# Running TensorE's head inside a two-pass loop so that the next instruction block is touched early

## Chip, cores and metric

One core of one Trainium2 chip. The metric is the device time of one execution in microseconds (us).

## The reference, cut to what matters

The reference is one decode step of a transformer block for 8 sequences: adaptive layer norm, grouped-query attention over a cache of 8,192 keys, and a dense layer with squared relu.

```python
# B = 8, D = 512, Hq = 32, Hkv = 8, Sk = 8192, Dh = 128, F = 1792; everything bf16
mod = silu(c) @ w_mod                              # 6 modulation vectors
q = (layernorm(x) * (1 + ca) + sa) @ wq
p = softmax(q @ k_cache^T * Dh ** -0.5)            # k_cache, v_cache: 134 MB each
x = x + ga * ((p @ v_cache) @ wo)
h = layernorm(x) * (1 + cb) + sb
x = x + gb * (relu(h @ w1 + b1) ** 2 @ w2 + b2)
```

The two caches are 268 MB of the 284 MB that have to be read.

## The kernel before

All engines run a recorded list of operations. On TensorE, VectorE and ScalarE the work of one sequence (a "batch") is the body of a loop of eight passes. Ahead of the loop stands the engine's head (modulation, q projection), behind it the tail (the end of the last batch, `wo`, `w1`, `w2`). The sync engine issues the loads, unrolled, into a ring of four 4 MiB slots.

```python
def _looped(self, e, eng, passes):
    nc, per, pe = self.nc, self.per[e], self.LOOP[e]
    seen, first = {}, {}
    for o in self._part(e, None):                       # the head
        self._emit(eng, o, self._want(e, o, 0), seen)
    # ... cut: waits that lie outside the loop are emitted here
    with nc.Fori(0, passes, engines=[pe], head_slot={pe: 0} if e == "tensor" else None) as i:
        for j, o in enumerate(self._part(e, (0, "a"))):
            self._emit(eng, o, first["a", j], seen)
        with eng.If(i < passes - 1):                    # the last pass leaves part b out
            # ... cut: part b, a drain, the semaphores set back by one pass
    for o in self._part(e, "post"):                     # the tail
        self._emit(eng, o, self._want(e, o, passes - 1), after)
```

`head_slot` pins the loop's first instruction at a slot of a block of 256 instructions, so that nothing ahead of the loop can shift its body. On TensorE the head has about 200 instructions, the body about 1,700, the tail about 580.

The tail ends with the dense layer. The last two loads are 512 KB and 256 KB of `w2`:

```python
d_w2 = [dma("sync", s_w2[i], ...) for i, (a, z, j) in
        enumerate(((0, 4, 4), (4, 8, 4), (8, 12, 4), (12, 14, 2)))]
...
for f in range(FT):                                     # FT = 14
    for k in range(KT):                                 # KT = 4
        t = op("tensor", lambda e, f=f, k=k: e.matmul(
            yT_ps[:, k, :], W2v[:, f, k * 128:(k + 1) * 128], hidT[:, f, :],
            start=False, stop=(f == FT - 1), ...), [k_sq[f // 7], d_w2[f // 4]])
```

## Time and profile before

| | before |
|---|---|
| time, median of the runs ahead of the prediction | 669.88 us (669.33 to 670.03) |
| span of the profiled run | 667.6 us |
| bytes moved | 283.85 MB, 425 GB/s over the span |
| TensorE busy | 77% of the span |
| DMA hardware queue | 99.1% of the 16 DMA engines' span |

From the page of the kernel before, the span and the DMA queues (packets, MB, share of the 16 engines' span):

```profile
span 667.6 us, 15485 instructions
...
## 3 DMA queue, kind: packets, MB, share of 16 engines
q1 hardware_dynamic: 12116, 283.65, 99.1%
q8 instruction: 9, 0.15, 0.1%
```

Queue q1 is the kernel's own loads. Queue q8 carries instructions: nine packets of 16,384 bytes, each 1.02 to 1.10 us long. From the instruction records I work out when they come: the first begins after TensorE enters the loop, and the other eight each after TensorE has gone through another 256 of the recorded instructions that follow, counted in program order (the body has 1,696). So I read a packet as one block of 256 TensorE instructions, and speak of a boundary at each 256th and of the fetch that it triggers. That a fetch brings the block after the one just entered is my reading too: when a packet of pass 1 begins, TensorE has already begun 19 to 111 instructions behind the boundary.

The windows view of the kernel before (stretch and its length in us; busy time of each engine; the last three columns are TensorE's granted clock, the DMA share and GB/s):

```profile
27.00:105.00 78.00, 59.24 (x804) 41.17 (x804) 35.70 (x64) 31.52 (x35) 0.00 (x0) 0.89 1.00 425
339.00:417.00 78.00, 62.32 (x840) 41.86 (x840) 36.59 (x66) 31.52 (x35) 0.00 (x0) 0.89 1.00 432
646.00:668.00 22.00, 14.17 (x304) 9.47 (x296) 6.13 (x22) 0.64 (x2) 0.00 (x0) 0.72 0.73 291
```

In a batch of 78 us the DMA share is 1.00 and TensorE is busy for about 60 us. The waits view of the kernel before (us in total, times, longest) says the same from the other side:

```profile
PE PS L479 <- DMA ring<-in_A_k_cache_dram: 51.2, 9, 10.1
PE PS L616 <- DMA ring<-in_A_v_cache_dram: 45.9, 10, 6.5
```

TensorE waits for keys and values, not they for it. Two stretches remain, the start and the end. The timeline of TensorE at the start (start us, length us, what, and in brackets the idle time before it and what ended it):

```profile
4.52 0.29 PE L373 MATMUL PS<-IDENT,KTb 8*128 8x8 bf16 x4 [4.52 <-DVE KTb L369]
...
11.33 3.21 PE L398 MATMUL PS<-ring,KTb 128*32 128x512 bf16 x24
...
30.71 1.04 PE L479 MATMUL PS<-IDENT,ring 128*128 128x128 bf16 x8 [5.12 <-DMA ring<-in_A_k_cache_dram]
```

The end, from the timeline of the kernel before:

```profile
661.68 1.02 PE L751 MATMUL PS<-KTb,ring 128*128 128x8 bf16 x32 [0.98 <-DVE KTb L747]
...
663.57 1.01 PE L751 MATMUL PS<-KTb,ring 128*128 128x8 bf16 x24 [0.87 <-DMA ring<-in_B_w_dram]
```

The last 24 `w2` matmuls wait 0.87 us for data. What follows them takes 3 us (a VectorE step, transposes, a copy, the output). The critical view (the chain of work that ended last: start us, length us, what) shows that the last eight of them stand directly behind the landing of the last load:

```profile
649.42 14.74 DMA ring<-in_B_w_dram
664.16 0.05 issue
664.21 0.39 PE PS L751 x8
```

The trace also records every DMA packet. I read two things from these records, which no view of the profile prints. They are worked out, not lines of the profile.

```
instruction fetches, kernel before, us:
 31.80  42.42  50.93  69.86  77.61  86.85  102.89      652.52  661.23
last w2 landing, by engine, us (the six latest of 16; the very last is the engine of the 661.23 fetch):
 662.21 662.22 662.46 662.67 662.71                     663.74
```

The engine of the last fetch has its `w2` packets behind that fetch. It ends at 663.74 us, 1.0 us after all others. These are the landings of two tiles, engine by engine, as distance from a straight line of 9.7115 us a tile (worked out from the packet records); the fetch at 102.89 us lies between them:

```
tile 9,  us: 0.63 0.73 0.74 0.75 0.80 0.87 1.04 1.31 1.51 1.69 2.15 2.16 2.16 2.17      2.63 2.66
tile 10, us: 0.62 0.73 0.75 0.76 0.80      1.03 1.30 1.50 1.68 2.15 2.16 2.16 2.17 2.42 2.63 2.65
```

One engine has gone from 0.87 to 2.42 us, the others stand. A tile counts as landed when the last of its 16 engines is done: above, TensorE's last eight matmuls start at 664.21 us, although 15 engines had written their share by 662.71 us.

### The profile page before, as it was taken

To read this page: it belongs to the slowest core of one execution; us is meant where nothing else is said; L and a number is where in the kernel's file an instruction comes from. 1 tells how busy PE (TensorE), PEld (TensorE's weight loads), DVE (VectorE), ACT (ScalarE), POOL (GpSimd) and SP (SyncE) were. 2 spreads that over 40 slices of the span, in tenths; PEclk is the share of its full clock that TensorE was granted. 3 is DMA by queue.
4 is the path that set the end of the run, shared out by engine and by line. 5 is a ranking of instruction groups with operands and counts; after the bars stand their busy time and mean duration, and the time that the engine had idled before them with its cause. 6 is when DMAs were issued, how large, how long until landed. Compare 5 with 4: busy or idle time off the path is not lost.

```text
span 667.6 us, 15485 instructions
## 1 busy us (share of the span) xinstructions
PE 513.8 (77%) x7064; PEld 344.8 (52%) x7064; DVE 302.6 (45%) x571; ACT 258.7 (39%) x289; POOL 18.4 (3%) x76
## 2 busy tenths in 40 slices
PE   3493984898739985699848987499756998389885
PEld 2283731675328742577317853287425773177534
DVE  2262731566216651367314662166513673156722
ACT  2151640466105660266404662066502654046610
POOL 7300000000000000000000000000000000000000
PEclk9696997899969998699977999699987999779996
DMA  9999999999999999999999999999999999999996
GB/s 376 431 412 437 426 427 435 432 430 430 434 434 430 430 432 436 428 432 432 436 428 430 434 434 430 430 434 434 428 432 434 434 426 434 432 434 428 434 415 264
DMA packets 12176, 283.85 MB, mean 425 GB/s; under 512 B 1250, under 2 KB 1283, under 8 KB 3588
## 3 DMA queue, kind: packets, MB, share of 16 engines
q1 hardware_dynamic: 12116, 283.65, 99.1%
q8 instruction: 9, 0.15, 0.1%
q10 hardware_dynamic: 48, 0.02, 0.0%
q14 instruction: 3, 0.02, 0.0%
HBM read 283.66 MB, written 0.01 MB: 425 GB/s over the span
## 4 chain that ended last, share of the span: by engine, by line
PE 52%; DMA 37%; ACT 7%; DVE 2%; SPq 1%; issue 1%
PE PS L479 36%; DMA ring<-in_A_k_cache_dram 32%; PE PS L496 9%; ACT P_sb L562 5%; PE PS L616 2%; DMA ring<-in_B_w_dram 2%; DMA ring<-in_A_wq_dram 2%; PE PS L469 1%; SPq L659 1%; ACT KTb L484 1%; DVE O_sb L626 1%; PE PS L463 1%; PE PS L574 1%; DVE Pm L588 0%; PE PS L594 0%
## 5 line engine op out<-in xcount | busy, mean ns | idle before, releaser
L484 ACT ACTIVATE KTb<-PS 128x1024 bf16<-128x1024 bf16 x192 | 196.5, 1024 | 332.2 <-PE PS L479 332.2
L479 PE MATMUL PS<-IDENT,ring 128*128 128x128 bf16 x4096 | 267.4, 227 | 51.2 <-DMA ring<-in_A_k_cache_dram 51.2
L479 PEld LDWEIGHTS PS<-IDENT,ring 128*128 128x128 bf16 x4096 | 246.8, 102 | 99.6 <-DMA ring<-in_A_k_cache_dram 52.4
L486 DVE COPY KTb<-PS 128x1024 bf16<-128x1024 bf16 x320 | 210.1, 687 | 143.9 <-PE PS L479 141.8
L616 PE MATMUL PS<-ring,Pm 128*32 128x512 bf16 x992 | 70.4, 434 | 46.8 <-DMA ring<-in_A_v_cache_dram 45.9
L496 PE MATMUL PS<-KTb,Qb 128*32 128x512 bf16 x1024 | 78.8, 385 | 4.5 <-ACT KTb L484 4.5
L626 DVE CAST O_sb<-PS 128x512 bf16<-128x512 f32 x31 | 21.4, 692 | 126.7 <-PE PS L616 126.7
L616 PEld LDWEIGHTS PS<-ring,Pm 128*32 128x32 bf16 x992 | 26.8, 106 | 85.5 <-DMA ring<-in_A_v_cache_dram 54.4
L562 ACT ACTIVATE P_sb<-PS,negm 128x1024 bf16<-128x1024 f32 x32 | 35.2, 1112 | 20.2 <-DVE negm L557 20.2
L469 PE MATMUL PS<-ONES 128*128 128x512 f32 x80 | 42.1, 630 | 0.0
L574 PE MATMUL PS<-IDENT,P_sb 128*128 128x128 bf16 x256 | 19.9, 220 | 15.4 <-ACT P_sb L562 15.4
L588 DVE COPY Pm<-PS 64x512 bf16<-64x512 bf16 x48 | 20.2, 421 | 25.0 <-PE PS L574 24.5
L574 PEld LDWEIGHTS PS<-IDENT,P_sb 128*128 128x128 bf16 x256 | 14.4, 98 | 25.1 <-ACT P_sb L562 25.1
L463 PE MATMUL PS<-IDENT 128*128 128x512 bf16 x88 | 26.9, 380 | 0.0
L496 PEld LDWEIGHTS PS<-KTb,Qb 128*32 128x32 bf16 x1024 | 15.4, 94 | 21.1 <-ACT KTb L484 8.5
L503 DVE TENSOR_REDUCE m<-PS 128x1 f32<-128x512 f32 x32 | 22.0, 689 | 6.6 <-PE PS L496 6.6
L630 PEld LDWEIGHTS PS<-SEL,O_sb 128*128 128x128 bf16 x124 | 5.8, 97 | 30.5 <-DVE O_sb L626 30.5
L469 PEld LDWEIGHTS PS<-ONES 128*128 128x128 f32 x80 | 12.7, 190 | 10.6 <-issue 10.6
L630 PE MATMUL PS<-SEL,O_sb 128*128 128x8 bf16 x124 | 7.9, 169 | 12.4 <-DVE O_sb L626 12.0
L641 DVE TENSOR_TENSOR oTn<-PS,rinv 128x8 f32 x31 | 6.0, 194 | 14.9 <-PE PS L630 14.9
L463 PEld LDWEIGHTS PS<-IDENT 128*128 128x128 bf16 x88 | 7.7, 105 | 9.1 <-issue 7.2
L484 ACT ACT_TABLE_LOAD x8 | 10.3, 1283 | 3.2 <-issue 3.2
(132 smaller groups left out, 115.9 us busy)
## 6 DMA issues: line engine op xcount, KB each, us to landing
ring<-in_A_k_cache_dram SPq DMA_DIRECT2D x32, 4096.0 KB, 34.2
ring<-in_A_v_cache_dram SPq DMA_DIRECT2D x31, 4096.0 KB, 27.8
ring<-in_A_wq_dram SPq DMA_DIRECT2D x1, 4096.0 KB, 19.9
wo_sb<-in_A_wo_dram SPq DMA_DIRECT2D x1, 4096.0 KB, 47.6
ring<-in_w_mod_dram SPq DMA_DIRECT2D x1, 3072.0 KB, 10.3
ring<-in_A_v_cache_dram SPq DMA_DIRECT2D x1, 2048.0 KB, 22.6
ring<-in_B_w_dram SPq DMA_DIRECT2D x3, 512.0 KB, 19.4
ring<-in_B_w_dram SPq DMA_DIRECT2D x1, 1344.0 KB, 17.9
```

Of the source, the lines that this page charges most:

```text
L463: ts = [op("tensor", lambda e: e.matmul(bank(at).rearrange("p (a r) -> p a r", a=4), IDENT[:, :], rhs)) for _ in range(n)]
L469: ts = [op("tensor", lambda e: e.matmul(bank(at).rearrange("p (a r) -> p a r", a=4), ONES[:, :], rhs)) for _ in range(n)]
L479: t = op("tensor", lambda e, j=j, i=i: e.matmul(STG[j][:, i, :], src[:, 32 * k + 8 * j + i, :], IDENT[:, :], is_transpose=True), [loaded[n ...
L484: stg_free[j] = op("scalar", lambda e, j=j, dst=dst: e.activation(dst, STG[j], ACT.Copy), [t])
L486: stg_free[j] = op("vector", lambda e, j=j, dst=dst: e.tensor_copy(dst, STG[j]), [t])
L496: t = op("tensor", lambda e, hf=hf, q=q, rhs=rhs: e.matmul(PS[32 * q:32 * (q + 1), k, :], Qb[:, 2 * p + hf, :], rhs, start=(p == 0 and hf ...
L503: return op("vector", lambda e: e.tensor_reduce(m4[:, k:k + 1], bank(k), AX.X, ALU.max), [t])
L562: exps.append(op("scalar", lambda e, k=k: e.activation(P_sb[:, k, :, :, :], bank(k).rearrange("p (i x) -> p i x", i=8).unsqueeze(2).to_bro ...
L574: t = op("tensor", lambda e, k=k, i=i: e.matmul(STG[k][:, i, :], P_sb[:, k, i, :, :].rearrange("p h x -> p (h x)"), IDENT[:, :], is_transp ...
L588: done.append(op("vector", lambda e, dst=dst, frm=frm: e.tensor_copy(dst, frm), [t, k_pm]))
L616: t = op("tensor", lambda e, p=p, m=m, cg=cg, vt=vt, Obank=Obank: e.matmul(Obank[32 * cg:32 * (cg + 1), :], lhs[:, p, 32 * m:32 * m + 32], ...
L626: t = op("vector", lambda e, osb=osb, Obank=Obank: e.tensor_copy(osb, Obank), [t])
```

## The change

The intent: make TensorE enter the block of the loop's body before the head's work begins, so that the block after it is fetched early and not when the loop starts. For that the head stands in a loop of two passes. Pass 0 skips the head and jumps to the first slot of the next block (this is what the alignment does), from where the loop's branch goes back. Pass 1 runs the head. The main loop's first instruction moves from slot 0 to slot 16, as the closing instructions of the new loop now have the first slots of that block.

```diff
-        for o in self._part(e, None):
-            self._emit(eng, o, self._want(e, o, 0), seen)
+        if e == "tensor":
+            with nc.Fori(0, 2, engines=[pe]) as i:
+                with eng.If(0 < i):
+                    for o in self._part(e, None):
+                        self._emit(eng, o, self._want(e, o, 0), seen)
+                eng.addr_align(bass.FETCH_BLOCK_INSTRUCTIONS, offset=0, max_nops=0)
+        else:
+            for o in self._part(e, None):
+                self._emit(eng, o, self._want(e, o, 0), seen)
 ...
-        with nc.Fori(0, passes, engines=[pe], head_slot={pe: 0} if e == "tensor" else None) as i:
+        with nc.Fori(0, passes, engines=[pe], head_slot={pe: 16} if e == "tensor" else None) as i:
```

## The prediction

> **What bounds the kernel now.** The DMA stream. The page's part 3 gives the hardware queue 99.1% of the 16 engines' span; the windows view shows DMA share 1.00 at 425 to 432 GB/s in every batch, TensorE busy 59 to 62 of 78 us. A 4 MiB tile lands every 9.71 us. TensorE waits for it (waits view: 51 us before key transposes, 46 us before value matmuls), so TensorE work or a branch inside the loop is off the critical path. Critical are the stream and what follows its last byte: the last `w2` landing is written at 663.7 us, the last 24 matmuls start at 663.57 us, the span ends at 667.6 us.

> **What the change does.** No arithmetic, wait or kernel DMA is added or removed. TensorE gets about ten control instructions; the loop body moves from slot 0 to slot 16 of its block. I count about 1,700 instructions, 7 blocks of 256 in both versions. Pass one jumps over the head, enters the body's first block, and jumps back. TensorE has nothing to do until 4.5 us (timeline), so the pass is free there if it takes under 3 us.

> What moves is an instruction fetch. [...] 9 packets of 16,384 bytes, at 31.8, 42.4, 50.9, 69.9, 77.6, 86.8, 102.9, 652.5, 661.2 us, none in passes 2 to 8, so the loop stays resident [...]. Each is one packet on one busy engine. From neighbouring packets' ends I work out that it sets that engine back about 1.07 us (its landings' phase goes from 0.66 to 1.69 us at the first), for good. Seven engines carry one each by 103 us. The fetch at 661.2 us hits an engine of that slow group ahead of its last `w2` packets: it ends at 663.74 us, the next slowest at 662.71 us. So 1.0 us of fetch is critical at the end.

> Entering the body's block near 1 us should bring the 31.8 us fetch to about 2 to 3 us, as the stream starts (first packet 1.84 us). If the engine still has idle startup time then, and is the one that takes the 661.2 us fetch (eight fetches later; the phases permit it), the end comes up to 1.0 us earlier. If the stream already runs, the same work is only done earlier: nothing gained. Estimate: 0 to 1.0 us, mean 0.4 us.

> **Predicted time.** 669.4 us, 8 in 10 between 668.6 and 670.2 us. Chances: faster by over 2% 0.005, within 2% 0.99, slower by over 2% 0.005.

> **What would show it.** Still 9 or 10 TensorE fetches; the first near 2 to 3 us, none near 31.8 us; later ones within 1 us of before. Tiles still every 9.71 us. The last `w2` landing between 662.7 and 663.8 us; TensorE's last wait for `w2` 0.87 us or less. Busy times the same.

> **What would make it wrong.** If slot 16 pushed the loop out of residence, fetches would appear in each pass: about 56 more, each 1.07 us on one of 16 engines, some 4 us. If the jump back refetches blocks, a few more, under 1 us. If an extra fetch shifts the engines' order, the last may fall on another engine, up to 1 us either way.

The forecast's sum came to a gain of 0 to 1.0 us, mean 0.4 us, and so to 669.4 us, from the 1.0 us by which the engine of the last fetch ends behind the next (663.74 and 662.71 us). That a fetch would follow the entry into the block within 1 to 2 us was my own estimate; the trace of the kernel before has 4.3 us.

## The result

| | before | after |
|---|---|---|
| time, median of 4 runs | 669.86 us (669.33 to 670.03) | 669.61 us (669.29 to 670.03) |
| ratio | | 0.9998 (95%: 0.9981 to 1.0015) |
| span of the profiled run | 667.6 us | 667.5 us |
| instruction fetches | 9 | 9 |

A ratio here is the mean time of one kernel's fast runs over that of the other's of the same rounds, so it is not quite the ratio of the medians in the table. The two kernels cannot be told apart.

From the page of the kernel after, span and queues:

```profile
span 667.5 us, 15496 instructions
...
## 3 DMA queue, kind: packets, MB, share of 16 engines
q1 hardware_dynamic: 12116, 283.65, 99.1%
q8 instruction: 9, 0.15, 0.1%
```

The windows view of the kernel after, the same stretches:

```profile
27.00:105.00 78.00, 60.72 (x804) 42.29 (x804) 36.00 (x68) 31.73 (x36) 0.11 (x1) 0.89 1.00 426
339.00:417.00 78.00, 61.62 (x840) 41.08 (x840) 36.47 (x66) 31.54 (x35) 0.00 (x0) 0.91 1.00 431
646.00:668.00 22.00, 14.28 (x304) 9.59 (x296) 6.12 (x22) 0.64 (x2) 0.00 (x0) 0.69 0.72 289
```

The waits view of the kernel after (its line numbers are 7 higher):

```profile
PE PS L486 <- DMA ring<-in_A_k_cache_dram: 50.0, 9, 9.0
PE PS L623 <- DMA ring<-in_A_v_cache_dram: 45.3, 10, 6.5
```

The start of the kernel after, from its timeline:

```profile
4.52 0.29 PE L380 MATMUL PS<-IDENT,KTb 8*128 8x8 bf16 x4 [4.52 <-DVE KTb L376]
...
11.83 3.60 PE L405 MATMUL PS<-ring,KTb 128*32 128x512 bf16 x24 [0.66 <-DMA ring<-in_w_mod_dram]
...
31.26 0.50 PE L486 MATMUL PS<-IDENT,ring 128*128 128x128 bf16 x3 [5.04 <-DMA ring<-in_A_k_cache_dram]
```

The end of the kernel after, from its timeline:

```profile
661.73 1.05 PE L758 MATMUL PS<-KTb,ring 128*128 128x8 bf16 x32 [0.97 <-DVE KTb L754]
...
663.43 1.01 PE L758 MATMUL PS<-KTb,ring 128*128 128x8 bf16 x24 [0.65 <-DMA ring<-in_B_w_dram]
```

Its critical view ends in the same way:

```profile
649.55 14.47 DMA ring<-in_B_w_dram
664.02 0.05 issue
664.07 0.39 PE PS L758 x8
```

The first matmul starts at 4.52 us in both: the extra pass is hidden. But the `w_mod` matmuls now wait for data and start 0.5 us later, and so do the first key transposes. The packet records show why:

```
instruction fetches, kernel after, us:
  6.29  42.99  51.09  69.79  78.34  85.54  100.41      652.37  660.00
last landing of the first tile (w_mod), slowest engine:  before 10.73 us, after 11.36 us
last w2 landing, slowest engine:                         before 663.74 us, after 663.61 us
```

The fetch of 31.8 us is gone and one at 6.29 us has come in its place. The slowest landing of `w_mod` is 0.6 us later. I read that as the engine of the fetch, and the runs below agree: it is 11.28 to 11.47 us in the five kept traces with an early fetch and 10.56 to 11.17 us in the eight without. The records of TensorE's control instructions date the cause: the jump to the next block is issued at 1.36 us, the first instruction there runs at 1.72 us, pass 1 reaches the head at 2.3 us. From 1.72 us to the transfer it is 4.6 us. In the kernel before the loop is entered at 27.47 us and the fetch begins at 31.80 us, 4.3 us later. So the early fetch met a stream that had been running since 1.84 us.

### The profile page after: what moved, and what is told of

Read it like the earlier page. It is cut to its first block, busy times and chain, and to the rows that moved or that the text cites. A ratio compares the mean times of both kernels' runs of the same rounds, so it can differ in the third digit from the quotient of the medians.

```text
span 667.5 us, 15496 instructions
## 1 busy us (share of the span) xinstructions
PE 515.8 (77%) x7064; PEld 345.8 (52%) x7064; DVE 302.4 (45%) x571; ACT 258.9 (39%) x289; POOL 18.6 (3%) x76
## 2 busy tenths in 40 slices
DMA packets 12176, 283.85 MB, mean 425 GB/s; under 512 B 1250, under 2 KB 1283, under 8 KB 3588
## 3 DMA queue, kind: packets, MB, share of 16 engines
q1 hardware_dynamic: 12116, 283.65, 99.1%
## 4 chain that ended last, share of the span: by engine, by line
PE 52%; DMA 36%; ACT 7%; DVE 2%; SPq 2%; issue 1%
PE PS L486 36%; DMA ring<-in_A_k_cache_dram 32%; PE PS L503 9%; ACT P_sb L569 5%; PE PS L623 2%; DMA ring<-in_B_w_dram 2%; DMA ring<-in_A_wq_dram 2%; SPq L666 1%; PE PS L476 1%; ACT KTb L491 1%; DVE O_sb L633 1%; PE PS L470 1%; PE PS L581 1%; DVE Pm L595 1%; PE PS L601 0%
## 5 line engine op out<-in xcount | busy, mean ns | idle before, releaser
L486 PEld LDWEIGHTS PS<-IDENT,ring 128*128 128x128 bf16 x4096 | 247.5, 103 | 98.8 <-DMA ring<-in_A_k_cache_dram 51.2
```

The lines of the kernel that those rows point to most:

```text
L486: t = op("tensor", lambda e, j=j, i=i: e.matmul(STG[j][:, i, :], src[:, 32 * k + 8 * j + i, :], IDENT[:, :], is_transpose=True), [loaded[n ...
```

## The experiments

Theory A: the kernel is bound by the DMA stream and by what follows its last byte. An instruction fetch is work on one DMA engine (at the fetch of 102.89 us one engine's landing went from 0.87 to 2.42 us, the others stood). Moved, it is the same work at another time, and only the last fetch lies on the critical path. Rival B: the early fetch did gain something, and slot 16 or the extra pass gave it back. Rival C: the end is set by TensorE's own tail, not by the last fetch.

### Slot 16 alone

The kernel before, with one edit:

```diff
-head_slot={pe: 0}
+head_slot={pe: 16}
```

> The kernel before with only the loop's head moved from slot 0 to slot 16, no two-pass loop. Theory A (the fetch only moved: DMA stream bound, a fetch sets one DMA engine back by the same amount wherever it falls): 669.3 to 670.1 us, ratio 1.000, 9 fetch packets with the first near 31.8 us, last w2 landing 663.6 to 663.8 us. Rival B (the early fetch gained something near 0.5 us and slot 16 or the extra pass gave it back): slot 16 alone is slower by about 0.5 us, or the two-pass loop alone is (next run).

Measured: 669.55 us (669.37 to 670.45, 5 runs) against 669.44 us before, ratio 1.0002 (0.9989 to 1.0016). Nine fetches, the first at 31.9 us, last `w2` landing 663.84 us (just above the range expected). Slot 16 by itself costs nothing that five rounds can see. One thing moved: the seventh fetch came at 100.5 us and not at 102.9. With slot 16 it came at 100.3 to 101.5 us in all six kept traces. The block boundary falls 16 instructions earlier in the pass there, which may be the reason. But a run with slot 0 (the 16-row loads below) had it at 101.5 us too, so a part can be the run.

### The extra pass without its touch

The changed kernel, with one edit; pass 0 then ends in the head's own block:

```diff
-                eng.addr_align(bass.FETCH_BLOCK_INSTRUCTIONS, offset=0, max_nops=0)
```

> The changed kernel without the alignment in the first pass, so that pass ends in the head's own block and touches no other. Theory A: the first fetch is back near 31.8 us, the tiles' front (first w_mod matmul) back near 11.3 us instead of 11.8 us, and the time is still 669.3 to 670.1 us. Rival B: the pass without its touch costs about 0.5 us or more.

Measured: 669.80 us (669.46 to 669.84, 5 runs), ratio 1.0001 (0.9988 to 1.0015). The first fetch is back at 31.9 us, the `w_mod` matmuls start at 11.24 us again, and the slowest `w_mod` landing is back at 10.86 us (10.73 before, 11.36 after). So it is the touch, not the pass, that moves the fetch and sets one engine of the first tile back, and neither moves the time. Rival B falls as far as 0.15% can show: no part of the change costs or gains 1 us.

### Ten passes in place of two

```diff
-            with nc.Fori(0, 2, engines=[pe]) as i:
-                with eng.If(0 < i):
+            with nc.Fori(0, 10, engines=[pe]) as i:
+                with eng.If(8 < i):
```

> The changed kernel with ten passes instead of two, nine of them skipping the head. Each skipping pass took about 0.95 us, so TensorE begins near 9 to 10 us instead of 2.3 us. Theory A: the w_mod matmuls start within 1.5 us of 11.8 us, all later landings and the time stay: 669.3 to 670.1 us, one early fetch only, since the touched block is there from the first pass on. If TensorE's front were critical: up to 7 us slower.

Measured: 669.97 us (669.65 to 670.26, 4 runs) against 669.37, ratio 1.0008 (0.9991 to 1.0025). One early fetch, at 6.39 us. A skipping pass takes 0.97 us. The first line of TensorE in the timeline of this run:

```profile
10.47 0.26 PE L380 MATMUL PS<-IDENT,KTb 8*128 8x8 bf16 x4 [10.47 <-POOL R L316]
```

TensorE begins at 10.47 us, not 4.52. (The view names a POOL instruction as what ended the idle time, but the last of TensorE's own branches is at 10.23 us; it is the skipping passes that end there.) The `w_mod` matmuls start at 13.64 us, the keys' first transposes at 31.37 us as in the kernel after. (The expectation of at most 1.5 us for the `w_mod` matmuls was a little low: it was 1.8.) The 6 us are swallowed before the loop starts; the median is 0.6 us up, within noise. This shows that neither the extra pass (1.4 us) nor a fetch stall of that size at TensorE's front can matter.

### The loop one block further on

The changed kernel, with one edit; as slot 0 of the touched block is taken, the body moves to the block after it:

```diff
-head_slot={pe: 16}
+head_slot={pe: 0}
```

> The changed kernel with the loop's head at slot 0: since the first pass ends in the body's old block, the body now starts one block later. Theory A: one fetch more, 10 packets; no fetches in passes 2 to 8; time within 669.2 to 670.4 us, because the fetch which is last then falls on one engine of the slow group as before. If each fetch were worth 1 us of time: 670.7 us.

Measured: 670.09 us (669.88 to 670.39, 4 runs) against 669.37, ratio 1.0009 (0.9992 to 1.0025). Ten fetches, two of them (6.38 and 32.69 us) ahead of the loop's second block, none in passes 2 to 8, and the last at 662.34 us. Within the range expected, but inconclusive between "no cost" and "up to 1 us": the spans were 668.5, 667.6, 667.9 and 667.7 us against 667.5 to 667.8 us before. In the profiled run, the 668.5 us one, the last landing was at 664.69 us, so there the last fetch hit an engine that ended later.

### The tail without the last fetch, and its control

Both runs are wrong on purpose (a part of the arithmetic is left out). In the first, 128 TensorE instructions of the tail are left out, so that the boundary that triggers the last fetch is reached only in the `w2` matmuls:

```diff
-        for g in range(6):                 # projection, start=(g == 0)
+        for g in range(5, 6):              # start=(g == 5)
-                for g in (6, 7):
+                for g in (7,):
-            for f in range(FT):            # w1 matmuls
+            for f in range(FT if k in (0, KT - 1) else 0):
```

> The changed kernel with 128 TensorE instructions of the tail left out (wrong result on purpose), so that the block boundary which triggers the last fetch is reached only in the w2 matmuls. Theory A: the fetch near 660 us comes after 662.3 us; the last w2 landing is at 662.7 to 662.9 us (the slowest engine without it) instead of 663.6 us; the span is 0.7 to 1.0 us shorter. Rival C (the end is set by TensorE's own tail, not by the fetch): it gets shorter about as much as the run with the short tail that keeps the fetch.

In the control only the third of these edits is made. Its 56 instructions stand behind the trigger, so the fetch stays while TensorE is early too:

> Control of the run before it: only the 28 w1 matmuls that stand behind the trigger are left out (wrong result on purpose), so TensorE reaches the w2 matmuls about 1 us sooner but the fetch near 660 us stays. Theory A: last w2 landing still 663.5 to 663.8 us, span within 0.2 us of before. Rival C: span shorter by about 0.5 to 1 us.

| | before | fetch out of the way | control, fetch stays |
|---|---|---|---|
| time, median | 669.44 us | 668.77 us (668.42 to 669.14) | 669.49 us (669.29 to 669.75) |
| ratio | | 0.9985 (0.9971 to 0.9999) | 0.9998 (0.9984 to 1.0012) |
| spans of the runs | 667.5 to 668.1 us | 666.6 to 667.1 us | 667.5 to 667.9 us |
| last fetch begins | 661.23 us | 662.25 us | 661.66 us |
| last `w2` landing | 663.74 us | 662.88 us | 663.61 us |

(The first column's fetch and landing are those of the profile before.) The `w2` matmuls in the timeline of the run without the fetch:

```profile
660.40 0.59 PE L758 MATMUL PS<-KTb,ring 128*128 128x8 bf16 x16 [0.84 <-DVE KTb L754]
661.49 0.59 PE L758 MATMUL PS<-KTb,ring 128*128 128x8 bf16 x16 [0.50 <-DMA ring<-in_B_w_dram]
662.71 1.01 PE L758 MATMUL PS<-KTb,ring 128*128 128x8 bf16 x24 [0.63 <-DMA ring<-in_B_w_dram]
```

The same matmuls in the timeline of the control:

```profile
661.27 1.02 PE L758 MATMUL PS<-KTb,ring 128*128 128x8 bf16 x32 [0.97 <-DVE KTb L754]
662.69 0.59 PE L758 MATMUL PS<-KTb,ring 128*128 128x8 bf16 x16 [0.41 <-DMA ring<-in_B_w_dram]
664.07 0.38 PE L758 MATMUL PS<-KTb,ring 128*128 128x8 bf16 x8 [0.79 <-DMA ring<-in_B_w_dram]
```

In both, TensorE is early and waits for `w2` at the end. The control leaves out fewer instructions (56, not 128), but as TensorE waits for data in both, what more the first one leaves out cannot be what it gains. The control's time is that of the kernel before, so a shorter TensorE tail alone buys nothing: rival C falls. (The last fetch of the first run came at 662.25 us, not after 662.3 as expected.) Without the fetch ahead of the last packets the landing comes 0.9 us earlier and every one of five spans is shorter than every span of the control. About 0.9 us of instruction fetch is on the critical path at the end, and it belongs to the last fetch. The change moves the first one.

### A body that does not stay resident

The kernel before, with one edit; the body then reaches into an eighth block:

```diff
-head_slot={pe: 0}
+head_slot={pe: 128}
```

> The kernel before with the head at slot 128: the body of about 1,700 instructions then reaches into an eighth block[...]. Theory A with loss of residence: about 8 fetches in each of the 8 passes, 60 to 70 packets in all. If they take turns on 8 engines, each gets about 7 more at 1.07 us: 676 to 679 us; if on all 16 engines, about 3.5 more each: 672 to 675 us. If the loop stays resident: 9 or 10 packets and no change.

(That residence might be lost was an assumption, to be tested here.)

Measured: 679.05 us (678.67 to 682.98, 4 runs), ratio 1.0161 (1.0129 to 1.0193). From the page of this run:

```profile
span 677.2 us, 15485 instructions
...
q1 hardware_dynamic: 12116, 283.65, 98.0%
q8 instruction: 55, 0.90, 0.6%
```

And from its waits view (TensorE's own wait ahead of the key transposes, for which the profile shows no releaser):

```profile
PE PS L479 <- issue: 46.9, 7, 9.5
PE PS L479 <- DMA ring<-in_A_k_cache_dram: 25.5, 4, 8.8
```

Fifty-five fetches and not nine. The branch back took 6.7 to 7.8 us in five passes, where it takes 0.21 to 0.23 us in the kernel before. These stalls of TensorE are mostly hidden: together they are 36 us, and its waits for keys have shrunk from 51.2 to 25.5 us. What costs time is told by the landings of one tile in the middle, engine by engine, again as distance from the straight line:

```
tile 35, before: 0.70 0.73 0.73 0.78 0.86 1.10 1.36 1.57 | 1.74 2.23 2.24 2.24 2.25 2.49 2.72 2.74
tile 35, slot 128: 0.57 0.64 0.67 0.82 1.18 1.23 1.46 1.58 | 6.75 6.79 6.90 6.96 7.25 7.83 9.06 10.20
```

### An attempt at a faster version, and its control

The experiments point to a kernel whose last fetch comes behind the stream. A correct way is to bring the boundary later. From the kernel before, ten of eleven bf16 filler matmuls and all five fp32 ones, which only keep TensorE busy, are left out of each pass, and the four `b2` matmuls are put directly ahead of the `w2` matmuls:

```diff
-            pe_stream32(1, 4)               # so at all places
-            pe_stream(1, 4)                 # so at all places but the next
 ...                                         # cut: the b2 matmuls, moved
-            turn_acts(pe_stream(3, 1))
+            turn_acts(pe_stream(1, 1))
```

> A correct attempt at a faster version, from the kernel before: ten of the eleven bf16 filler matmuls and all five fp32 ones of each pass are left out (40 instructions a pass) and the four b2 matmuls stand directly ahead of the w2 matmuls, so that the last block boundary is reached 48 instructions later, near 659.5 us. Theory A: with 2 to 4 us from boundary to transfer, the last fetch comes at 661.7 to 663.2 us; if it is after 662.3 us the last w2 landing is at 662.7 to 662.9 us and the time about 668.8 us, if before, 669.0 to 669.7 us. If the fillers are needed for the clock, the tail gets slower and hides it.

(The 2 to 4 us from boundary to transfer are an estimate; in the kernel before it was 2.3 to 3.5 us for the eight fetches behind the loop's entry.)

The control has the head at slot 48 in addition, to bring the boundary back:

> Control of the run before it: the same instructions, but the loop's head at slot 48, which brings the boundary back to the same place in the tail as in the kernel before. Theory A: last fetch at 660 to 661.8 us, last w2 landing 663.5 to 663.9 us, 669.3 to 670.0 us; what differs from the run before it is the fetch, what differs from the kernel before is the fillers.

Measured: 669.98 us (669.57 to 670.92), ratio 1.0009 (0.9995 to 1.0022), and for the control 669.70 us (669.25 to 670.55), ratio 1.0008 (0.9994 to 1.0021), against 669.44 us. Neither is faster. In both the last landing did come early (663.00 and 662.83 us; the control missed its expectation, its last fetch came at 662.09 us), but TensorE was no longer there to use it. The timeline of the first of the two:

```profile
650.16 2.15 PE L523 MATMUL PS<-wo_sb,KTb 128*32 128x512 bf16 x24 [0.50 <-DVE KTb L518]
...
664.43 1.66 PE L738 MATMUL PS<-KTb,ring 128*128 128x8 bf16 x56 [0.78 <-DVE KTb L730]
```

The same projection in the timeline of the kernel before:

```profile
648.64 1.48 PE L523 MATMUL PS<-wo_sb,KTb 128*32 128x512 bf16 x24 [0.51 <-DVE KTb L518]
```

The 24 projection matmuls took 2.15 us, not 1.48, and the `w2` matmuls start at 664.43 us without waiting for data. Mean granted clock was 0.84 in both kernels against 0.90 before, so leaving out fillers went with a lower granted clock. What the stream gained at the end, TensorE lost. That the lower clock alone made its tail late is not shown, as the `b2` matmuls were moved in both runs too.

### A second attempt: the last load on eight engines

If TensorE's fetches burden eight engines, the last load could go to the other eight. A load of 8 rows was expected to run on eight engines only; in the trace before, the two loads of 8 rows (`x` and `c`) show one increment of their semaphore at issue and eight as data lands, the 4 MiB loads 16 as data lands. From the kernel before, the 256 KB load at the end is issued in pieces of 8 rows, and in the control in pieces of 16 rows:

```diff
-    for i, (a, z, j) in enumerate(((0, 4, 4), (4, 8, 4), (8, 12, 4), (12, 14, 2)))]
+    for i, (a, z, j) in enumerate(((0, 4, 4), (4, 8, 4), (8, 12, 4)))]
+w2_l = B_w2[1536:1792].rearrange("(p j) n -> p j n", p=128, j=2)
+for r in range(0, 128, 8):                   # control: 16
+    d_l = dma("sync", s_w2[3], lambda e, r=r: e.dma_start(
+        W2v[r:r + 8, 12:14, :], w2_l[r:r + 8]))
+d_w2.append(d_l)
```

> A second correct attempt at a faster version, from the kernel before: the last w2 load (256 KB) is issued as 16 loads of 8 rows each. [...] A 16-engine share of this load takes one engine 0.65 us. If the eight are the ones without instruction fetches, the engine of the last fetch has 0.65 us less to do and the last w2 landing is near 663.1 us instead of 663.7: span 0.3 to 0.6 us shorter. If they are the eight with fetches, that engine has 0.65 us more: landing near 664.4 us, span 0.5 to 0.7 us longer. If they are four of each kind: about as when the engine of the last fetch is among them or not, either way.

> Control of the run before it: the last w2 load is issued as 8 loads of 16 rows[...]. Last w2 landing 663.6 to 663.9 us and span as in the kernel before, within 0.2 us, unless the extra issues themselves cost time.

(Which eight engines a load of 8 rows gets was an assumption. The 0.65 us can be read in the kernel before: eight packets of 2,048 bytes on an engine, at steps of 0.08 us.)

Measured: 671.01 us (670.82 to 672.27), ratio 1.0026 (1.0013 to 1.0040), and for the control 670.62 us (670.30 to 671.07), ratio 1.0018 (1.0004 to 1.0031). Both are slower, the control too, so the issue in pieces costs time by itself: 1.1 us with 8 pieces. The timeline of the run with 8 rows:

```profile
663.87 0.59 PE L756 MATMUL PS<-KTb,ring 128*128 128x8 bf16 x16 [1.16 <-DMA ring<-in_B_w_dram]
665.73 0.38 PE L756 MATMUL PS<-KTb,ring 128*128 128x8 bf16 x8 [1.26 <-DMA ring<-in_B_w_dram]
```

The last write of data in the packet records is at 663.50 us, 0.2 us earlier than before, but TensorE's last eight matmuls start at 665.73 us, 2.2 us after it. With 16 rows these are 664.02 and 665.05 us, 1.0 us apart. In the kernel before the same distance is 0.5 us (663.74 to 664.21 us). The time goes between the last landing in the packet records and TensorE's release. The trace's records of the semaphore show where: with 16 rows its last increments arrive 0.15 us apart, up to 665.00 us, while the packets that carry them end 0.085 us apart. Why they arrive more slowly than they are sent, no run shows.

The same records answer a part of the question for which the run was made. With 8 rows the semaphore counts 16 increments while the loads are issued and 128 as data lands, and the page has 112 more packets under 512 bytes than before (1,362 and 1,250), which is 16 times eight less the 16 of the one load. So I conclude that each of the 16 loads ran on eight engines. The engine of the last fetch (661.62 to 662.80 us) carries none of their packets: its last one ends at 663.22 us, where in the kernel before that engine ended at 663.74 us. So it was relieved by 0.5 us, as hoped. But each of the eight other engines carried two shares, and the last of them ended at 663.50 us. Whether the remaining fetches also go to engines outside these eight, I did not work out. No version here beats the two kernels.

## Why the prediction was right

The forecast of the time, "within 2%", rests on the mechanism and not on luck: one fetch moves inside a stream that sets the time. The range of 668.6 to 670.2 us says less. It holds both branches of the prediction, a gain of 1.0 us and none, and a mean gain of 0.4 us is below what the runs resolve (about 0.15%, or 1 us). The packet records, not the time, tell the branches apart.

- **Bound by the DMA stream: right.** Same bytes, the same DMA share of 1.00, and the ten-pass run shows 6 us of TensorE's front to be free.
- **The change moves one fetch and nothing else: right.** Nine fetches in both, the one of 31.8 us gone, none in passes 2 to 8, the loop resident at slot 16 as at slot 0. Here a body in seven blocks was fetched once (9 packets), one that reaches into an eighth again and again (55 packets), though not after the sixth branch back. Why the limit lies there, no run shows.
- **The size of the gain: the term that was mis-sized.** The prediction said that the fetch should come "at about 2 to 3 us, as the stream starts" and gave "0 to 1.0 us, mean 0.4 us". It came at 6.29 us, 4.6 us after the jump landed, when the engine had no startup time left. The first tile's slowest landing went from 10.73 to 11.36 us: the fetch still set an engine back. Its second branch, "the same work is only done earlier: nothing gained", is what the runs showed. The latency was in the trace before: the loop was entered at 27.47 us and the fetch began at 31.80 us. I had not read it there. It is not a constant: between TensorE's entry by a jump or at the loop's start and the transfer lie 3.1 to 5.0 us in the 13 kept traces, 3.1 and 4.3 us in the two kernels with split loads, which are the same up to that point.
- **"Later ones within 1 us of before": wrong in three of eight.** The fetches at 86.8, 102.9 and 661.2 us came 1.3, 2.5 and 1.2 us earlier. The run with slot 16 alone has the seventh at 100.5 us too, so for that one it may be the slot (see there).
- **1.0 us of fetch is critical at the end: right, and shown.** The run without it is 0.9 us shorter, its control is not. The prediction's further guess, that this engine is also the one of the first fetch, is only argued: both end in the same group of landings. No run settles it.
- **"About 1.07 us" for a fetch: mis-sized.** It is 1.5 us. I had compared two sorted lists of landings and paired the wrong engines at the first fetch (0.66 with 1.69 us, where 0.17 fits the lists). The packets agree with 1.5: the fetch at 102.89 us took 1.07 us itself, and the packet behind it 0.5 us more than its neighbours. What counts at the end is the 1.0 us by which that engine is later than the next.
- **What a lost residence would cost ("some 4 us"): wrong.** It cost 9.6 us, as the fetches go to eight engines and not to 16, and each costs 1.5 us.

## What to carry to other kernels

In this stream-bound kernel an instruction fetch was work on one DMA engine, and moving it inside the stream moved nothing. Taken behind the last packets of its engine, the last fetch no longer cost its 0.9 us; a fetch ahead of the first byte was never reached, so what that would gain is not shown. Look for the last thing that delays the last packet, not for the first stall of the engine. And before counting on an early prefetch, read from the trace how long after its trigger a fetch begins, and compare that with the time at which the stream starts.
